# RWKV-5 attention followed by a balanced expert layer on one core: the first expert's list and gather move ahead of a branch, and the attention's preparation returns into its arm

## The chip, the core and the metric

The kernel runs on one core of a Trainium2 chip. A core has five engines with their own instruction queues: TensorE (PE, whose weight loads are shown as PEld), VectorE (DVE), ScalarE (ACT), GpSimd (POOL) and SyncE (SP), which here only issues transfers. ACT and POOL issue transfers too. The time of a run is the device's time in microseconds; the kernel before has a median of 490.0 us over three runs (488.75 to 490.1).

## The reference

Two layers follow each other. The first is a linear attention with a decaying state, for 4 batches, 8 heads, 768 steps and heads of 48 numbers. The second sends each of the resulting 3072 tokens to one of 8 experts, each of which gets exactly 384.

```python
for t in range(S):
    kt, vt, rt = (k[:, :, t], v[:, :, t], r[:, :, t])
    cur = np.einsum('bhd,bhe->bhde', u[None] * kt, vt)
    y[:, :, t] = np.einsum('bhd,bhde->bhe', rt, state + cur)
    state = w[None, :, :, None] * state + np.einsum('bhd,bhe->bhde', kt, vt)
...
x = attn_out.transpose(0, 2, 1, 3).reshape(B * S, H * D)
logits = x @ w_gate
for idx in np.argsort(-logits.flatten()):
    tok, e = (int(idx) // E, int(idx) % E)
    if assigned[tok] >= 0 or counts[e] >= cap:
        continue
    assigned[tok] = e
    counts[e] += 1
...
for e in range(E):
    mask = assigned == e
    h = np.maximum(x[mask] @ w1[e], 0.0)
    out[mask] = h @ w2[e]
```

So a pair of token and expert with a high logit is served first, and an expert that has 384 tokens takes no more. An expert that has filled up is closed, its tokens are struck out, and the rest of the tokens look again among the experts left. All is 32-bit floating point.

## The kernel before, in words

**The attention** works in 24 units, each of 128 steps of one batch with all 8 heads. Heads lie in pairs, each padded to 64 columns, so that a pair fills 128. For a unit n the parts are:

- `load(n)` brings k, r and v (192 KB each) with three transfers on SP's queue.
- `scale(n)` multiplies k by powers of w (`ks`, L395, VectorE), forms the sums r·u·k by head (`rk` on POOL, L398 and L399; `dd` on VectorE, L401), and fills the diagonal of `AT` from `dd` with eight instructions on ScalarE (L404).
- `turn(n)` transposes r and ks by pairs of heads on TensorE (L414, L417). VectorE multiplies the turned r by powers of w as it takes it out of PSUM (L419), ScalarE copies the turned k (L421).
- `pairs(n)` multiplies both (g, 16 products, L460) and puts the upper triangle into `AT` (masking, L463, VectorE).
- `outputs(n)` sums state times r (L475) and AT times v (L479) into y_ps, with weights of 48 columns; ScalarE copies it to `xT` (L482). The state takes up `kv_ps` (L490, L496, L497), for all but a batch's last chunk.
- `rows(n)` turns xT back (L506), ScalarE copies it (L508), and SP stores it to `x_rows`. `gate(c)` computes the logits of a chunk of all batches.

Iteration n of the loop (L528) traces scale(n+2), turn(n+1), pairs(n+1), outputs(n) and rows(n-1). The order on each engine's queue is not the order of the text: a planner draws it at compiling, with its own costs of instructions, from what is ready. A branch (`tc.If`) is for the planner one piece that other work may stand before or behind, but not inside. `tc.issue_after(ins)` puts instructions behind `ins` on its engine.

The class `Mild` prepares tables from w: `up` on VectorE and `ch` on POOL, both by doubling (L334 to L342), a reciprocal (L343), and a table `wk` turned by TensorE (L360). It also holds scale(0), turn(0) and scale(1), ahead of the branch that asks whether w lies in a range; here it does, and `attention_mild` is the arm that runs.

**The experts.** For each expert `walk.fill()` makes a search, the likely one (`likely`): three rounds of 16 thresholds. In each, VectorE compares (`ind`, line L706 of a helper, as are many others), TensorE counts (L718, then L729), VectorE sums in between (`own`, `cnt`, `wide`). Out of the last come the expert (`fmax`), its tokens (`acc`), their places and a flag that says whether the search is sure. Then:

1. Every engine reads the flag and takes the branch (L742); only if it is 0, `surely` searches by bits.
2. `tokens(place)` turns places into a list `tok` (L944 to L973), with VectorE and two groups of products on TensorE.
3. `leave` strikes the expert and its tokens out of the logits (L755 to L760).
4. `fetch` gathers 3 x 128 rows of `x_rows` by `tok` (POOL, L1043), and has SP read the expert's number and load w1 (L1035) and w2 (L1037), 1.5 MB each, one behind the other on SP's queue.

`turn(xg)` transposes the rows (L1053, L1054), `hidden` makes the first layer (L1062, L1063), `result` the second (L1069, L1071), and POOL scatters the rows to the output (L1072). The search, the list and the fetch of expert n+1 are traced ahead of `hidden` of expert n. Before the first expert there is nothing to lie beside.

Of the kernel before, what the change touches and what calls it, by code (L numbers as in the profile page):

```python
# [10 lines left out]
F32 = mybir.dt.float32  # L11
BF16 = mybir.dt.bfloat16
F16 = mybir.dt.float16
I32 = mybir.dt.int32
# [12 lines left out]
def attention_any(ctx, kpads, rpads, tc, r, k, v, w, u, wg, x_dram, LG, ident, walk):  # L27
# [22 lines left out]
    NB = len(kpads)  # L50
# [224 lines left out]
class Mild:  # L275
# [6 lines left out]
    def __init__(self, ctx, tc, r, k, v, w, u, wg, ident):  # L282
# [9 lines left out]
        self.tc, self.r, self.k, self.v, self.ident = tc, r, k, v, ident  # L292
        const = self.const = ctx.enter_context(tc.tile_pool(name="m_const", bufs=1))
        self.pool = ctx.enter_context(tc.tile_pool(name="m_work", bufs=2))
        self.units = [(b, c) for c in range(C) for b in range(B)]
        self.loaded, self.live, self.marks = {}, {}, {}

        flat = w.rearrange("h d -> (h d)")
        row = const.tile([1, DX], F32, name="row")
        wp = const.tile([P2, 8, HP], F32, name="wp")  # L300
        nc.vector.memset(wp[:, 0, :], 1.0)
        with nc.allow_non_contiguous_dma(reason="a row to the partitions"):
            for q in range(2):
                nc.scalar.dma_start(wp[q * PD:q * PD + D, 0, :], w.rearrange("(a q) d -> q d a", q=2)[q])
        nc.sync.dma_start(row, flat.unsqueeze(0))


        self.vts, self.rts, self.kss = (
            [const.tile([128, H, PD], F32, name=f"{name}{i}") for i in range(n)]
            for name, n in (("vt", 8), ("rt", 6), ("ks", 4)))  # L310
        for i in range(8):
            for t in (self.rts, self.vts, self.kss):
                if i < len(t):
                    (nc.vector if i < 2 else nc.gpsimd).memset(t[i][:, :, D:PD], 0.0)
        self.wg_sb = const.tile([128, HP, 32], F32, name="wg_sb")
        nc.vector.memset(self.wg_sb, 0.0)
# [3 lines left out]
        for n in range(1, 4):  # L320
            self.load(n)
        for q in range(2):
            nc.scalar.dma_start(self.wg_sb[q * PD:q * PD + D, :, 0:E],
                                wg.rearrange("(a q d) e -> q d a e", q=2, d=D)[q])

# [19 lines left out]
        self.wr = const.tile([P2, HP, T], F32, name="wr")  # L345
        nc.scalar.copy(self.wr, ch[:, :, T + 1:1:-1])
        self.wp = wp
        mask = const.tile([128, 128], F32, name="mask_f")
        make_upper_triangular(nc, mask, val=1.0, diag=False)
        self.mask = const.tile([128, 128], U8, name="mask")  # L350
        nc.gpsimd.tensor_copy(self.mask, mask)

# [762 lines left out]
```

## Time and profile before

| | before |
|---|---|
| median of runs | 490.0 us (488.75 to 490.1) |
| profiled execution | 490.1 us |
| its span, first to last instruction | 488.4 us |
| TensorE busy, instructions | 420.4 us (86%), 2896 |
| VectorE busy | 199.7 us (41%) |
| ScalarE busy | 149.7 us (31%) |
| POOL busy | 120.3 us (25%) |
| first product g of unit 0 starts | 17.36 us |
| last unit's xT copied out of PSUM | 173.19 us |
| first search starts (m) | 179.04 us |
| first expert product starts | 210.44 us |
| read from HBM, written | 44.25 MB, 9.44 MB |

The profile is of one execution. Its times count from the first instruction, so that the span lies some 1.7 us below the execution's own time. The attention goes to about 175 us, the handover from 179 to 210, the eight experts from there to the end. Waits are put down to what released them; idle time on an engine that others do not wait for costs nothing.

### The profile page before, as it was taken

The page shows a single profiled execution, that of the slowest core. Times are in us where ns is not written, and L with a number is a line of the kernel's source. Part 1 is how long each engine was busy: PE and PEld are TensorE (multiplying, and loading weights), DVE is VectorE, ACT ScalarE, POOL GpSimd, SP SyncE. Part 2 cuts the span into 40 slices and gives each one's busy share as a digit, 9 for nine tenths or more (in the row PEclk, how much of TensorE's full clock was granted, in tenths as well). Part 3 has the DMA queues.
Part 4 walks back from the last instruction along what each step waited for, and adds up shares of the span by engine and source line. Part 5 has one row for each costly group of instructions (what it writes and reads, how often), then busy time and mean ns, then how long its engine had stood idle before and what let it go on. Part 6 is the DMA issues. An engine that isn't in the chain of part 4 may idle for free. (4 is left out here: it accounts for less than half of the span.)

```text
span 488.4 us, 7858 instructions
## 1 busy us (share of the span) xinstructions
PE 420.4 (86%) x2896; PEld 275.2 (56%) x2896; DVE 199.7 (41%) x673; ACT 149.7 (31%) x389; POOL 120.3 (25%) x178
## 2 busy tenths in 40 slices
PE   0798989899988631189999999999999999999994
PEld 0677767777776520145655655655656556556552
DVE  6775657555663327444045064072270350300000
ACT  2845546655556510012121121121221221212210
POOL 5914563444440000202102102203103112201001
PEclk9999999999999975569999999999999999999999
DMA  8986545555201010716203505307209019510000
GB/s 163 200 165 140 122 109 107 124 127 126 71 34 36 33 39 1 261 46 237 103 17 129 212 17 209 132 17 279 77 2 322 32 52 398 182 32 32 17 16 32
DMA packets 93960, 54.36 MB, mean 111 GB/s; under 512 B 77137, under 2 KB 88530, under 8 KB 93906
## 3 DMA queue, kind: packets, MB, share of 16 engines
q1 hardware_dynamic: 89858, 44.05, 32.1%
q0 software_dynamic: 3072, 9.44, 5.3%
q8 instruction: 27, 0.44, 0.4%
q10 hardware_dynamic: 976, 0.21, 0.3%
q14 instruction: 27, 0.22, 0.1%
HBM read 44.25 MB, written 9.44 MB: 110 GB/s over the span
## 5 line engine op out<-in xcount | busy, mean ns | idle before, releaser
L1062 PE MATMUL h_ps<-xT,w 128*128 128x384 f32 x384 | 137.5, 506 | 1.4 <-ACT xT L1054 0.5
L1069 PE MATMUL o_ps<-w,hid 128*128 128x384 f32 x384 | 127.5, 486 | 0.0
L1069 PEld LDWEIGHTS o_ps<-w,hid 128*128 128x128 f32 x384 | 71.9, 190 | 47.2
L1062 PEld LDWEIGHTS h_ps<-xT,w 128*128 128x128 f32 x384 | 69.5, 194 | 45.9 <-issue 10.6
L404 ACT ACTIVATE AT<-ident,dd 128x128 f32<-128x128 f32 x192 | 58.6, 388 | 59.2 <-PE y_ps L479 59.2
L1063 ACT ACTIVATE hid<-h_ps 128x384 f32<-128x384 f32 x64 | 31.4, 491 | 109.5 <-PE h_ps L1062 107.1
L1043 POOL DMA_INDIRECT xg<-x_rows,tok x24 | 23.3, 971 | 161.9 <-PE h_ps L1062 63.5
L1072 POOL DMA_INDIRECT out_dram<-o_sb,tok x24 | 23.7, 989 | 127.6 <-ACT o_sb L1071 122.4
L706 DVE TENSOR_TENSOR own<-counts,same 128x64 f32<-128x64 f32 x21 | 4.7, 225 | 102.0 <-PE counts L718 102.0
L1071 ACT COPY o_sb<-o_ps 128x384 f32<-128x384 f32 x24 | 11.5, 479 | 108.3 <-PE o_ps L1069 100.2
L475 PE MATMUL y_ps<-rT,state 128*48 128x128 f32 x320 | 31.0, 287 | 13.6 <-ACT xT L482 13.6
L398 POOL TENSOR_TENSOR rk<-rt,kt 128x384 f32<-128x384 f32 x24 | 24.8, 1033 | 66.7 <-DVE dd L401 38.8
L463 DVE COPY_PREDICATED AT<-mask,g_ps 128x512 f32<-128x512 uint8 x48 | 32.3, 725 | 19.4 <-ACT AT L404 17.8
L479 PE MATMUL y_ps<-AT,vt 128*48 128x128 f32 x384 | 32.8, 281 | 0.0
L475 PEld LDWEIGHTS y_ps<-rT,state 128*48 128x48 f32 x320 | 20.0, 126 | 20.9 <-issue 13.8
L460 PE MATMUL g_ps<-rT,kT 48*128 48x128 f32 x384 | 28.8, 291 | 2.3 <-DVE AT L463 1.5
L460 PEld LDWEIGHTS g_ps<-rT,kT 48*128 48x128 f32 x384 | 24.2, 193 | 7.0 <-issue 6.7
L479 PEld LDWEIGHTS y_ps<-AT,vt 128*48 128x48 f32 x384 | 25.1, 126 | 1.4 <-ACT xt L508 0.4
L399 POOL TENSOR_TENSOR rk<-rk,u_bc 128x384 f32<-128x384 f32 x24 | 25.6, 1070 | 0.5
L395 DVE TENSOR_TENSOR ks<-kt,wk 128x384 f32<-128x384 f32 x24 | 18.1, 762 | 13.6 <-PE kv_ps L490 13.5
L414 PE MATMUL rT_ps<-ident,rt 128*128 128x128 f32 x96 | 16.7, 297 | 6.3 <-DMA rt<-in_r_dram 6.3
L1054 ACT COPY xT<-xT_ps 128x384 f32<-128x384 f32 x24 | 10.9, 486 | 35.9 <-PE counts L718 32.1
(170 smaller groups left out, 405.2 us busy)
## 6 DMA issues: line engine op xcount, KB each, us to landing
w<-in_moe_w_dram SPq DMA_DIRECT2D x16, 1536.0 KB, 7.4
kt<-in_k_dram SPq DMA_DIRECT2D x24, 192.0 KB, 3.0
rt<-in_r_dram SPq DMA_DIRECT2D x24, 192.0 KB, 3.2
vt<-in_v_dram SPq DMA_DIRECT2D x24, 192.0 KB, 3.4
x_rows<-xt SPq DMA_DIRECT2D x24, 192.0 KB, 1.9
xg<-x_rows,tok POOLq DMA_INDIRECT x24, 6.3
out_dram<-o_sb,tok POOLq DMA_INDIRECT x24, 2.6
u_bc<-in_u_dram ACTq DMA_DIRECT2D x1, 192.0 KB, 3.7
```

The source lines that it names most:

```text
L398: nc.gpsimd.tensor_mul(rk, rt[:, :, 0:D], kt)
L399: self.marks["rk"] = nc.gpsimd.tensor_mul(rk, rk, self.u_bc.rearrange("p (h d) -> p h d", h=H)).ins
L404: nc.scalar.activation(AT[:, h % 2, h // 2, :], self.ident, AF.Copy, scale=dd[:, h:h + 1])
L460: g = nc.tensor.matmul(g_ps[:, q, a, :], kT[halves[q], a, :], rT[halves[q], a, :], start=True, stop=True)
L463: marks["AT"] = nc.vector.copy_predicated(out=AT[:, q], mask=mask.unsqueeze(1).to_broadcast([128, HP, T]), data=g_ps[:, q]).ins
L475: nc.tensor.matmul(y_ps[halves[q], a, :], S0[:, a, q, 0:D], rT[:, a, :], start=(a == 0), stop=False, skip_group_check=True)
L479: nc.tensor.matmul(y_ps[halves[q], a, :], vt[:, 2 * a + q, 0:D], AT[:, q, a, :], start=(c == 0 and a == 0), stop=(a == HP - 1), skip_group ...
L1043: nc.gpsimd.indirect_dma_start(out=xg[:, c, :], out_offset=None, in_=x_dram, in_offset=bass.IndirectOffsetOnAxis(ap=tok[:, c:c + 1], axis=0))
L1062: nc.tensor.matmul(h_ps, w1[:, f, ts(j, 128)], xT[:, f, :], start=(f == 0), stop=(f == KD - 1))
L1063: nc.scalar.activation(hid[:, j, :], h_ps, AF.Relu)
L1069: nc.tensor.matmul(o_ps, hid[:, j, ts(c, 128)], w2[:, j, :], start=(j == 0), stop=(j == KF - 1))
L1072: nc.gpsimd.indirect_dma_start(out=out_rows[n * NC + c], out_offset=bass.IndirectOffsetOnAxis(ap=tok[:, c:c + 1], axis=0), in_=o_sb, in_of ...
```

## The change

It has two sides. On the experts' side:

- `tokens` and the gather (now `rows`) are traced ahead of reading the flag, for the likely search's places, and once more inside the branch's arm, into the same tiles, behind `surely`.
- `leave` follows the branch, and thus the list.
- In `likely`, `eq`, `low`, `base`, `em` and `past_low` are put behind `ind` or `wide` (`issue_after`), where VectorE waits for counts; the flag goes behind `place`.
- For the first expert alone, w2 is issued by ScalarE, behind the copy of the first turned rows, and not by SP behind w1.

On the attention's side:

- scale(0), scale(1) and turn(0) go from `Mild`, ahead of the branch, into `attention_mild`.
- r is scaled on VectorE before it is turned (`rs`, from a table `wr` that is turned like `wk`), and ScalarE copies the turned r. The rows `xt` are copied by VectorE instead of ScalarE.
- y_ps is written with weights of 64 columns, pads included, and is allocated in each unit; its one memset goes.
- In `Mild`, 12 pads are cleared on VectorE (before, 18 on VectorE and POOL), w's transfer `wp` is traced behind them, behind the mask and behind the filling of the states. Three units are loaded ahead, not four; v has 6 tiles, not 8.
- `attention_any` makes its own padded tiles; this arm does not run.

The diff, cut to its core:

```diff
+        self.vts, self.kss, self.rss = (
+            [const.tile([128, H, PD], F32, name=f"{name}{i}") for i in range(n)]
+            for name, n in (("vt", 6), ("ks", 4), ("rs", 2)))
+        for t in self.vts + self.kss + self.rss:
+            nc.vector.memset(t[:, :, D:PD], 0.0)
...
+        self.state = [const.tile([128, HP, 2, PD], F32, name=f"state{b}") for b in range(B)]
+        for t in self.state:
+            nc.scalar.activation(t.rearrange("p a q d -> p a (q d)"),
+                                 ident.unsqueeze(1).to_broadcast([128, HP, 128]), AF.Copy, scale=0.0)
+        self.wg_sb = const.tile([128, HP, 32], F32, name="wg_sb")
+        nc.vector.memset(self.wg_sb, 0.0)
         flat = w.rearrange("h d -> (h d)")
...
         wp = const.tile([P2, 8, HP], F32, name="wp")
         nc.vector.memset(wp[:, 0, :], 1.0)
         with nc.allow_non_contiguous_dma(reason="a row to the partitions"):
             for q in range(2):
                 nc.scalar.dma_start(wp[q * PD:q * PD + D, 0, :], w.rearrange("(a q) d -> q d a", q=2)[q])
...
-        self.vts, self.rts, self.kss = (
-            [const.tile([128, H, PD], F32, name=f"{name}{i}") for i in range(n)]
-            for name, n in (("vt", 8), ("rt", 6), ("ks", 4)))
-        for i in range(8):
-            for t in (self.rts, self.vts, self.kss):
-                if i < len(t):
-                    (nc.vector if i < 2 else nc.gpsimd).memset(t[i][:, :, D:PD], 0.0)
-        self.wg_sb = const.tile([128, HP, 32], F32, name="wg_sb")
-        nc.vector.memset(self.wg_sb, 0.0)
         self.u_bc = const.tile([128, DX], F32, name="u_bc")
         self.load(0)
         nc.scalar.dma_start(self.u_bc, u.rearrange("h d -> (h d)").partition_broadcast(128))
-        for n in range(1, 4):
-            self.load(n)
         for q in range(2):
             nc.scalar.dma_start(self.wg_sb[q * PD:q * PD + D, :, 0:E],
                                 wg.rearrange("(a q d) e -> q d a e", q=2, d=D)[q])
+        for n in range(1, 3):
+            self.load(n)
...
-            self.scale(0)
-            self.turn(0, ps)
-            self.scale(1)
...
+        turned = const.tile([P2, HP, T], F32, name="turned")
+        nc.scalar.copy(turned, ch[:, :, T + 1:1:-1])
+        self.wp, self.scales = wp, []
+        with tc.tile_pool(name="m_ps", bufs=2, space=PSUM) as ps, ExitStack() as part:
+            for name, t in (("wk", ch), ("wr", turned)):
+                sc_ps = ps.tile([128, HP, P2], F32, name="sc_ps")
+                for a in range(HP):
+                    nc.tensor.transpose(sc_ps[:, a, :], t[:, a, 0:T], ident[0:P2, 0:P2])
+                sc = const.tile([128, DX], F32, name=name)
+                nc.scalar.copy(sc.rearrange("p (h d) -> p h d", h=H),
+                               sc_ps.rearrange("p a (q d) -> p (a q) d", q=2)[:, :, 0:D])
+                self.scales.append(sc)
...
-        nc.vector.tensor_mul(ks[:, :, 0:D], kt, self.wk.rearrange("p (h d) -> p h d", h=H))
...
-        rT = pool.tile([128, HP, T], F32, name="rT", bufs=3)
-        nc.vector.tensor_mul(rT, rT_ps, self.wr)
-        kT = pool.tile([128, HP, T], F32, name="kT")
-        nc.scalar.copy(kT, kT_ps)
...
-    halves = [slice(q * PD, q * PD + D) for q in range(2)]
-    y_ps = ps.tile([128, HP, T], F32, name="y_ps")
-    nc.vector.memset(y_ps, 0.0)
-    turned = {}
...
+    def scale(n):
+        load(n + 3)
+        kt, rt, vt = loaded.pop(n)
+        ks, rs = kss[n % 4], rss[n % 2]
+        nc.vector.tensor_mul(ks[:, :, 0:D], heads(kt), heads(wk))
+        nc.vector.tensor_mul(rs[:, :, 0:D], heads(rt), heads(wr))
+        rk = pool.tile([128, DX], F32, name="rk")
+        nc.gpsimd.tensor_mul(rk, rt, kt)
+        marks["rk"] = nc.gpsimd.tensor_mul(rk, rk, u_bc).ins
+        dd = pool.tile([128, H], F32, name="dd")
+        nc.vector.tensor_reduce(out=dd, in_=heads(rk), axis=AX.X, op=ALU.add)
+        AT = pool.tile([128, 2, HP, T], F32, name="AT", bufs=3)
+        for h in range(H):
+            nc.scalar.activation(AT[:, h % 2, h // 2, :], ident, AF.Copy, scale=dd[:, h:h + 1])
+        live[n] = dict(vt=vt, ks=ks, rs=rs, AT=AT)
+    def turn(n):
+        ks, rs = live[n]["ks"], live[n]["rs"]
+        kT_ps = ps.tile([128, HP, T], F32, name="kT_ps")
+        for a in range(HP):
+            nc.tensor.transpose(kT_ps[:, a, :], pair(ks, a), ident)
+        rT_ps = ps.tile([128, HP, T], F32, name="rT_ps")
+        for a in range(HP):
+            nc.tensor.transpose(rT_ps[:, a, :], pair(rs, a), ident)
+        kT = pool.tile([128, HP, T], F32, name="kT")
+        nc.scalar.copy(kT, kT_ps)
+        rT = pool.tile([128, HP, T], F32, name="rT", bufs=3)
+        nc.scalar.copy(rT, rT_ps)
+        live[n].update(kT=kT, rT=rT)
...
+        y_ps = ps.tile([128, HP, T], F32, name="y_ps")
         if c > 0:
             for a in range(HP):
                 for q in range(2):
-                    nc.tensor.matmul(y_ps[halves[q], a, :], S0[:, a, q, 0:D], rT[:, a, :],
+                    nc.tensor.matmul(y_ps[halves[q], a, :], S0[:, a, q, :], rT[:, a, :],
                                      start=(a == 0), stop=False, skip_group_check=True)
         for a in range(HP):
             for q in range(2):
-                nc.tensor.matmul(y_ps[halves[q], a, :], vt[:, 2 * a + q, 0:D], AT[:, q, a, :],
+                nc.tensor.matmul(y_ps[halves[q], a, :], vt[:, 2 * a + q, :], AT[:, q, a, :],
...
-                        nc.tensor.matmul(kv_ps[halves[q], a, :], ks[:, 2 * a + q, 0:D], vt[:, 2 * a + q, 0:D],
+                        nc.tensor.matmul(kv_ps[halves[q], a, :], ks[:, 2 * a + q, :], vt[:, 2 * a + q, 0:D],
...
-        nc.scalar.copy(xt.rearrange("p (h d) -> p h d", h=H),
-                       xr_ps.rearrange("p a (q d) -> p (a q) d", q=2)[:, :, 0:D])
+        nc.vector.tensor_copy(heads(xt), xr_ps.rearrange("p a (q d) -> p (a q) d", q=2)[:, :, 0:D])
...
+    scale(0)
+    scale(1)
+    turn(0)
     pairs(0)
     for n in range(N):
         if n + 2 < N:
-            mild.scale(n + 2)
+            scale(n + 2)
         if n + 1 < N:
-            mild.turn(n + 1, ps)
+            turn(n + 1)
...
-        tt(ind, self.by_token(m, ND), self.by_expert(cand), ALU.is_ge)
+        self.asked = tt(ind, self.by_token(m, ND), self.by_expert(cand), ALU.is_ge)
...
+        self.summed = tt(wide, digit_of.unsqueeze(2).to_broadcast([128, ND, E]),
...
         flag = self.likely(**out)
+        tok, listed = self.tokens(out["place"])
+        got = fetch(tok)
         found = nc.values_load(flag[0:1, 0:1], min_val=0, max_val=1,
                                skip_runtime_bounds_check_because="a truth value")
         with self.tc.If(found < 1):
             with ExitStack() as part:
                 pool = part.enter_context(self.tc.tile_pool(name="surely", bufs=1))
                 self.surely(pool, **out)
-        tok = self.tokens(out["place"])
+            self.tokens(out["place"], tok)
+            fetch(tok, got)
         self.leave(out["fmax"], out["acc"])
-        return out["fmax"], tok
+        return out["fmax"], tok, got
...
             if g == 0:
-                eq = pool.tile([128, NT, E], F32, name="eq")
-                tt(eq, prop, self.by_expert(self.first_e), ALU.mult)
-                em = pool.tile([128, NT], F32, name="em")
-                nc.vector.tensor_reduce(out=em, in_=eq, axis=AX.X, op=ALU.max)
+                with self.tc.issue_after(self.asked):
+                    eq = pool.tile([128, NT, E], F32, name="eq")
+                    tt(eq, prop, self.by_expert(self.first_e), ALU.mult)
+            else:
+                with self.tc.issue_after(self.asked):
+                    was, low = low, pool.tile([128, 1], F32, name="low")
+                    nc.vector.scalar_tensor_tensor(out=low, in0=self.cell[:, g - 1:g], scalar=dg, in1=was,
+                                                   op0=ALU.mult, op1=ALU.add)
+            with self.tc.issue_after(self.summed):
+                if g < 2:
+                    base = pool.tile([128, ND], F32, name="base")
+                    nc.vector.tensor_scalar(out=base, in0=self.cells[:, g + 1, :], scalar1=low, scalar2=None,
+                                            op0=ALU.add)
+                else:
+                    em = pool.tile([128, NT], F32, name="em")
+                    nc.vector.tensor_reduce(out=em, in_=eq, axis=AX.X, op=ALU.max)
+                    past_low = pool.tile([128, 1], F32, name="past_low")
+                    tt(past_low, low, self.cell[:, 2:3], ALU.subtract)
             if g < 2:
-                base = pool.tile([128, ND], F32, name="base")
-                nc.vector.tensor_scalar(out=base, in0=self.cells[:, g + 1, :], scalar1=low, scalar2=None, op0=ALU.add)
                 most = pool.tile([128, ND], F32, name="most")
...
-                was, low = low, pool.tile([128, 1], F32, name="low")
-                nc.vector.scalar_tensor_tensor(out=low, in0=self.cell[:, g:g + 1], scalar=dg, in1=was,
-                                               op0=ALU.mult, op1=ALU.add)
...
-        flag = pool.tile([128, 1], I32, name="flag")
-        nc.vector.scalar_tensor_tensor(out=flag, in0=upto[:, NT - 1:NT], scalar=float(CAP), in1=n_sole,
-                                       op0=ALU.is_equal, op1=ALU.mult)
-        tt(upto, upto, st_ps[:, 1, :], ALU.add)
-        nc.vector.scalar_tensor_tensor(out=place, in0=upto, scalar=128.0, in1=acc, op0=ALU.add, op1=ALU.mult)
+        before = pool.tile([128, NT], F32, name="before")
+        tt(before, upto, st_ps[:, 1, :], ALU.add)
+        placed = nc.vector.scalar_tensor_tensor(out=place, in0=before, scalar=128.0, in1=acc,
+                                                op0=ALU.add, op1=ALU.mult).ins
+        with self.tc.issue_after(placed):
+            flag = pool.tile([128, 1], I32, name="flag")
+            nc.vector.scalar_tensor_tensor(out=flag, in0=upto[:, NT - 1:NT], scalar=float(CAP), in1=n_sole,
+                                           op0=ALU.is_equal, op1=ALU.mult)
...
+    def rows(tok, xg=None):
+        if xg is None:
+            xg = xpool.tile([128, NC, DX], F32, name="xg")
+        for c in range(NC):
+            nc.gpsimd.indirect_dma_start(
+                out=xg[:, c, :], out_offset=None, in_=x_dram,
+                in_offset=bass.IndirectOffsetOnAxis(ap=tok[:, c:c + 1], axis=0))
+        return xg
+    def fetch(fmax, tok, xg, late=False):
         number = xpool.tile([1, 1], I32, name="number")
         nc.vector.tensor_scalar(out=number, in0=fmax[0:1, :], scalar1=-1.0, scalar2=float(E),
                                 op0=ALU.mult, op1=ALU.add)
-        e = nc.values_load(number[0:1, 0:1], engines=(mybir.EngineType.SP,), min_val=0, max_val=E - 1,
+        queues = (mybir.EngineType.SP, mybir.EngineType.Activation)
+        e = nc.values_load(number[0:1, 0:1], engines=queues if late else queues[:1], min_val=0, max_val=E - 1,
                            skip_runtime_bounds_check_because="E less a number from 1 to E")
         w1 = wpool.tile([128, KD, F], F32, name="w1")
         nc.sync.dma_start(w1, moe_w1[ds(e, 1)].rearrange("o (c p) f -> p (o c) f", p=128))
         w2 = wpool.tile([128, KF, DX], F32, name="w2")
-        nc.sync.dma_start(w2, moe_w2[ds(e, 1)].rearrange("o (c p) d -> p (o c) d", p=128))
-        return w1, w2
...
-    def turn(xg):
+        queue = nc.scalar if late else nc.sync
+        second = lambda: queue.dma_start(w2, moe_w2[ds(e, 1)].rearrange("o (c p) d -> p (o c) d", p=128))
+        if not late:
+            second()
+        return xg, tok, w1, w2, second
+    def turn(xg, second=None):
         xT = xpool.tile([128, KD, CAP], F32, name="xT")
         for c in range(NC):
             xT_ps = ps_t.tile([128, KD, 128], F32, name="xT_ps")
             for f in range(KD):
                 nc.tensor.transpose(xT_ps[:, f, :], xg[:, c, ts(f, 128)], ident)
-            nc.scalar.copy(xT[:, :, ts(c, 128)], xT_ps)
+            copied = nc.scalar.copy(xT[:, :, ts(c, 128)], xT_ps)
+            if c == 0 and second:
+                with tc.issue_after(copied.ins):
+                    second()
...
-    ahead = fetch(*walk.fill())
-    xT = turn(ahead[0])
+    ahead = fetch(*walk.fill(rows), late=True)
+    xT = turn(ahead[0], ahead[-1])
     for n in range(E):
-        _, tok, w1, w2 = ahead
+        _, tok, w1, w2, _ = ahead
         if n + 1 < E:
-            ahead = fetch(*(walk.fill() if n + 2 < E else walk.remainder()))
+            ahead = fetch(*(walk.fill(rows) if n + 2 < E else walk.remainder(rows)))
```

## The prediction

> **What bounds the kernel now.** I read the table of stages first, then the timeline of the handover between attention and experts, then one cycle of the attention and the list of waits, last the first 18 us.
>
> The stages (columns: window, its length, then busy us and instructions of PE, PEld, DVE, ACT, POOL, granted clock, DMA share, GB/s):
>
> ```profile
> 88.00:116.00 28.00, 26.00 (x361) 20.44 (x359) 16.28 (x31) 16.91 (x52) 12.15 (x17) 1.00 0.57 124
> 180.00:190.00 10.00, 1.80 (x12) 0.82 (x13) 7.37 (x31) 0.00 (x0) 0.00 (x0) 0.50 0.00 0
> 190.00:200.00 10.00, 1.35 (x13) 0.73 (x12) 7.99 (x40) 0.00 (x0) 0.57 (x1) 0.50 0.10 20
> 200.00:210.00 10.00, 2.80 (x14) 1.92 (x13) 2.43 (x10) 1.05 (x3) 2.50 (x3) 0.50 0.94 356
> 245.00:280.00 35.00, 34.61 (x131) 19.94 (x130) 13.30 (x61) 6.61 (x14) 5.92 (x6) 1.00 0.35 125
> ```
>
> Three regimes. From 210 on, TensorE works 34.6 of 35 us for each expert: nothing on other engines can shorten it. From 179 to 210 nothing overlaps: VectorE chooses the first expert's tokens, then DMA brings rows and weights. Up to 175 the attention runs at 26 of 28 us of TensorE, so it is close to that engine but not against it.
>
> The handover:
>
> ```profile
> 191.82 0.16 DVE L828 SCALAR_TENSOR_TENSOR flag<-upto,n_sole 128x1 int32<-128x1 f32 x1
> 192.22 0.18 DVE L831 SCALAR_TENSOR_TENSOR place<-upto,acc 128x24 int32<-128x24 f32 x1
> 193.87 0.18 DVE L944 TENSOR_SCALAR lo<-place 128x24 int32<-128x24 int32 x1 [1.46 <-DVEq L742]
> ...
> 197.55 0.42 SPq L1035 DMA_DIRECT2D w<-in_moe_w_dram  x1
> ...
> 198.22 0.15 DVE L973 TENSOR_REDUCE tok<-mine 128x3 int32<-128x12 f32 x1
> ...
> 199.43 1.17 POOL L1043 DMA_INDIRECT xg<-x_rows,tok  x1 [52.43 <-DVE cnt L725]
> ...
> 206.53 0.90 PE L1053 MATMUL xT_ps<-ident,xg 128*128 128x128 f32 x3 [6.46 <-DMA xg<-x_rows,tok]
> ```
>
> The branch costs VectorE 1.46 us, the list 4.50 (193.87 to 198.37), the first gathered rows 7.10 from their issue. The first expert matmul starts at 210.44, released by the last turned rows.
>
> One attention cycle (6.45 us, or 6.97 with a gate in it):
>
> ```profile
> 107.11 2.45 ACT L404 ACTIVATE AT<-ident,dd 128x128 f32<-128x128 f32 x8 [3.03 <-PE y_ps L479]
> 108.63 0.56 DVE L395 TENSOR_TENSOR ks<-kt,wk 128x384 f32<-128x384 f32 x1 [1.32 <-PE kv_ps L490]
> 109.29 1.34 DVE L463 COPY_PREDICATED AT<-mask,g_ps 128x512 f32<-128x512 uint8 x2
> 109.46 0.56 ACT L482 COPY xT<-y_ps 128x512 f32<-128x512 f32 x1
> 110.16 1.05 PE L475 MATMUL y_ps<-rT,state 128*48 128x128 f32 x14 [0.66 <-ACT xT L482]
> 111.14 1.16 PE L460 MATMUL g_ps<-rT,kT 48*128 48x128 f32 x16
> ```
>
> A loop: outputs end (107.07), ScalarE fills AT (2.45), copies xT (0.56), TensorE runs the state products, g and the outputs (3.4). The list of waits for 32 to 150 us says the same: "ACT AT L404 <- PE y_ps L479: 50.9, 18, 3.7" and only 9.4 us of TensorE behind xT. Masking ends at 110.63, 0.5 before g.
>
> **What the skill says.** "TensorEngine Tiling (Array Packing)", Available Configurations: without row tiling a weight of up to 64 columns takes one of two 128x64 tiles, and tiles work in parallel. The trace agrees: 16 products of 48 columns and 128 moving ones take 1.2 to 1.3 us, 8 pairs of 0.15, what one transpose of the full array takes (four in 0.60). So 48 and 64 columns should cost alike. "TensorE: Matmul & The Clock Gate", LDWEIGHTS: a load costs by its columns. The rows have 126 ns for 48 columns and 190 for 128, so some 139 for 64, an estimate; the loads lie beside the matmuls. "DMA: Bandwidth & Descriptors", Queues, rings and completion order: each DMA engine takes turns between queue rows by packets. Before, both weight matrices are on one queue; no row here shows the two sharing.
>
> **The change, part by part: the experts' side.**
> - Side values: eq and em leave the front (179.82 to 180.48: 0.66); low leaves two rounds (0.13 each). They go behind ind or wide, where VectorE waits for TensorE 0.4 to 0.6 us anyway; only em with past_low (0.5) overfills the last such wait of 0.36, giving back 0.1. Flag goes behind place: 0.19, of which it takes 0.13 again ahead of the list. So the list can start at 192.40 - 0.66 - 0.26 + 0.1 - 0.19 + 0.13 = 191.5 instead of 193.87, since the branch (1.46) is behind it.
> - The list loses its fill-ins: fe 0.14, dead 0.27, m about 0.15, ind about 0.4, so 3.5 rather than 4.5. tok at 195.0 instead of 198.37.
> - Gather: POOL began 1.06 after tok here, 0.27 at the next expert. Issued at 195.3 to 196.1, I take 195.7; the others 1.25 apart. With no weights in the way I price a landing by the scatters' 2.6 (median on the page) up to 3.2: the last rows at 201, turned by 203.
> - The weights lose: VectorE passes the branch after tok (0.84 to 1.46, to 196.2), strikes out (about 1.2), SP reads the number (1.0): w1 issued at 198.4, 0.9 later. It has 1.57 MB; at 356 GB/s 4.4 and about 2 to land: 204.8. w2, issued by ScalarE behind the first turned rows (about 200.5), halves it from 201.5 in the worst case: 207.1. I take 205.8, later than xT: w1 becomes the last thing. w2 has 20 us of first-layer work over it; without that cover it would cost some 3.
> - First expert matmul at 205.8 instead of 210.4: 4.6 gained, bounds 3.3 and 6.0 (207.1, 204.4).
> - The later seven searches do the same work under 34.6 of 35 us of TensorE: nothing. Without that cover the same 4 us a search would count. The gathers issue earlier on POOL, whose queue has only scatters behind them, and these wait for o_sb. The branch's arm now lists and gathers again, but no row of it runs in this trace.
>
> **The attention's side, taken back.**
> - The head: before, w's powers are ready when wp has landed (5.95), reciprocal ends at 9.99, POOL's ch at 12.77 (rk in between), and g of unit 0 starts at 17.36, 4.6 later. After, 13 memsets of 0.14 precede wp's own, so its transfer starts near 2.9, or behind ACT's table load and four state fills (1.28 + 4 x 0.55) near 5; it lands 4.2 later, 7.2 to 9.6. 4.0 to the reciprocal and 0.4 more for ch: 11.6 to 14.0. Then one scale more is turned (1.11 + 0.48) and r multiplied before its transposes, partly beside the other, 6.2 rather than 4.6: 17.8 to 20.2, and 2.4 later if AT of unit 1 is ahead of the copies of kT and rT on ACT. Units 0 to 2 then follow as before. I take 20.0: 2.7 lost, bounds 0.4 and 5.3. The arm's branch costs nothing visible before (ACT goes from AT to AT without a gap there), up to 1.5 in the worst case, within the bounds. Loads: three units ahead instead of four; with units 6.5 apart and landings of 3.0 to 3.4 this is 19 us early: nothing.
> - The cycle: VectorE loses rT (0.69, out of PSUM), gains rs (0.56 alone; ks, its like, averages 0.76) and xt (0.48). ACT loses xt (0.48), gains rT (0.57): the order AT, xT, kT, rT ends at 111.0, still before g's 111.14. kv with 64 columns: 0.1 in TensorE's 0.66 of slack. But rs comes behind ks, and ks ends at 109.19 with masking waiting behind it: it then ends 0.56 to 0.76 later, 111.2 to 111.4, and g waits 0.15 to 0.35. In three cycles of four (in a gate cycle ks is elsewhere): 0.19 on average, times 22: 4.1 lost. Bounds: -0.66 a cycle if another order frees TensorE from xT (its idle), +0.6 if ACT's two copies come ahead of xT too: -14 and +13.
> - y_ps memset (0.48) leaves: hidden before behind kT. The last xt on VectorE instead of ACT: same 0.48.
>
> Sum: -4.6 + 2.7 + 4.1 = +2.2. On the profiled execution (490.1, span 488.4 and 1.7 around it) 492.3; the median of the runs is 490.0, hardly different.
>
> **Rivals.** Less than 0.3% (1.5 us) can't be told from no change here.
> - Main, slower: 489.5 to 496, likeliest 492.3. Chance 0.42.
> - A. The attention loop doesn't notice: rs fits before masking or behind it, and the head costs 1 to 2 as the old interleaving of rk with ch on POOL was itself slow. For it: g had 0.5 us of slack; against: ks already fills the space to masking. -4.6 + 1.5 = 487, faster. It decides when the cycle stays under 6.55. Chance 0.30.
> - B. The cycle grows by 0.4 to 0.6, as rT's copy and xT compete on ACT ahead of g: -4.6 + 2.7 + 11 = 499. For it: ACT in order is the loop's longest part; against: it idles 2.7 each cycle. Chance 0.18.
> - C. The order drawn at compiling lets AT or g of the next unit run before the outputs end: -0.5 a cycle, 490 - 11 - 2 = 477 to 483. AT has three buffers yet waits for the outputs just ended, so there is room. Chance 0.07.
> - D. The early gather brings nothing, since rows wait for the arm that may write them too and for w1 behind w2: 210 as before, with the attention's loss 495 to 497. Chance 0.03.
>
> Faster: C, A without its near-zero part, a little of main: 0.33. Within 0.3%: the meeting of A and main, 0.17. Slower: 0.50. The range of 8 in 10 leaves out C and the upper half of B: 484 to 500; the main case's own is 489.5 to 496.
>
> **What would show it.** Right: first gather near 195.7 on the shifted clock, that is 17 us after the first m instead of 20.4; first expert matmul 27 after it instead of 31.4, released by w1; g of unit 0 near 20; cycle 6.6 with g waiting for masking; experts at 34.6 of 35. Wrong: a cycle below 6.4 or above 6.9, gathers still at 7 us to landing, or an expert's period other than 34.5 to 35.

## The result and the profile after

The kernel after takes 471.32 us (median; 468.33 to 471.97) beside 489.73 us for the kernel before, a ratio of 0.9615 (95% interval 0.9571 to 0.9659). It is faster by 3.9%; 492.3 had been forecast, with a range of 484 to 500.

The profiled executions took 490.1 and 471.97 us, their spans 488.4 and 470.2. I cut both spans at the same five events, read from the timelines: the end of the last output product of unit 3 and of unit 23, the first search's first instruction (m), the first expert product.

| stretch | before | after | difference | forecast |
|---|---|---|---|---|
| start to the outputs of unit 3 | 39.50 | 44.53 | +5.0 | +2.7 |
| 20 cycles, units 4 to 23 | 133.07 (6.65 each) | 113.09 (5.65 each) | -20.0 | +4.1 for 22 |
| outputs of unit 23 to m | 6.47 | 5.71 | -0.8 | 0 |
| m to the first expert product | 31.40 | 32.02 | +0.6 | -4.6 |
| first expert product to the end | 277.95 | 274.88 | -3.1 | 0 |
| sum | 488.4 | 470.2 | -18.2 | +2.2 |

All of the gain and more is in the attention's cycle. Of the other four stretches, the handover (m to the first expert product) went the other way from what I had written, and the experts, for which I had forecast nothing, gained 3.1 us.

**The stages after**, in the columns of the table of before (window, length, busy us and instructions of PE, PEld, DVE, ACT, POOL, clock, DMA share, GB/s):

```profile
88.00:116.00 28.00, 26.68 (x399) 23.82 (x396) 21.66 (x41) 18.23 (x52) 17.79 (x21) 1.00 0.64 137
164.00:174.00 10.00, 1.79 (x12) 0.82 (x13) 8.12 (x34) 0.00 (x0) 0.00 (x0) 0.50 0.01 2
174.00:184.00 10.00, 1.09 (x11) 0.87 (x11) 7.07 (x33) 0.00 (x0) 3.00 (x3) 0.50 0.13 28
184.00:194.00 10.00, 2.85 (x14) 1.64 (x13) 2.45 (x10) 1.44 (x3) 0.27 (x1) 0.50 0.93 348
245.00:280.00 35.00, 34.85 (x138) 20.06 (x137) 14.51 (x63) 6.60 (x14) 5.95 (x6) 1.00 0.35 125
```

The busy time of TensorE in the first window hardly moved (26.00 to 26.68 of 28), but it issued 399 matmuls where there were 361. I had read 26 of 28 as close to the engine's limit; a busy PE had not meant a PE at its peak.

**One cycle after**, from the timeline:

```profile
82.61 0.58 ACT L492 COPY xT<-y_ps 128x512 f32<-128x512 f32 x1 [2.76 <-PE y_ps L489]
83.09 2.45 ACT L444 ACTIVATE AT<-ident,dd 128x128 f32<-128x128 f32 x8
83.73 1.34 DVE L472 COPY_PREDICATED AT<-mask,g_ps 128x512 f32<-128x512 uint8 x2
84.41 1.09 PE L485 MATMUL y_ps<-rT,state 128*64 128x128 f32 x16
85.44 0.57 ACT L457 COPY kT<-kT_ps 128x512 f32<-128x512 f32 x1
85.90 0.58 ACT L459 COPY rT<-rT_ps 128x512 f32<-128x512 f32 x1
86.54 1.16 PE L469 MATMUL g_ps<-rT,kT 48*128 48x128 f32 x16
```

Before, ScalarE filled AT (2.45) and only then copied xT, so the state products waited for both. Now xT comes first, AT is filled behind it, for a unit three further on (unit 12, beside the xT of unit 9), whose masking comes only at 95.14. The lists of waits over the cycles say where the loop went. The first line before (32 to 165 us; total, times, longest):

```profile
ACT AT L404 <- PE y_ps L479: 56.5, 20, 3.7
```

The first two after (32 to 140 us):

```profile
POOL rk L438 <- DMA rt<-in_r_dram: 37.4, 17, 7.7
ACT xT L492 <- PE y_ps L489: 29.2, 10, 4.9
```

AT's wait for the output products is gone; where ScalarE waits for them now, it is to copy xT. Why AT waited can be read from the addresses of the built program. Before, `Mild` allocates AT with bufs=3 in a pool that is opened outside the branch, and fills units 0 and 1 ahead of the branch. Those two buffers are read inside the arm, and in the arm they are never given out again: AT of all the units 2 to 23 has one address. After, the pool is opened in the arm and three addresses rotate. (kT too has one address before, and rT two; e3 below leaves these as they are.)

**The head**, ScalarE's rows of the timeline of after:

```profile
15.28 0.58 ACT L457 COPY kT<-kT_ps 128x512 f32<-128x512 f32 x1 [1.27 <-PE kT_ps L452]
18.30 4.79 ACT L444 ACTIVATE AT<-ident,dd 128x128 f32<-128x128 f32 x16 [2.44 <-DVE dd L441]
23.00 0.56 ACT L459 COPY rT<-rT_ps 128x512 f32<-128x512 f32 x1
```

g of unit 0 starts at 23.61 (17.36 before). r is turned by 16.05, but ScalarE's queue has sixteen AT fills ahead of the copy, and the first of them waits for dd until 18.30.

**The handover after:**

```profile
175.47 0.18 DVE L856 SCALAR_TENSOR_TENSOR place<-before,acc 128x24 int32<-128x24 f32 x1
...
175.68 0.18 DVE L975 TENSOR_SCALAR lo<-place 128x24 int32<-128x24 int32 x1
...
179.17 0.17 DVE L1005 TENSOR_REDUCE tok<-mine 128x3 int32<-128x12 f32 x1
180.39 1.16 POOL L1064 DMA_INDIRECT xg<-x_rows,tok  x1 [38.23 <-DVEq L760]
...
182.44 0.43 SPq L1077 DMA_DIRECT2D w<-in_moe_w_dram  x1
183.13 1.14 POOL L1064 DMA_INDIRECT xg<-x_rows,tok  x1 [0.30 <-issue]
183.71 0.90 PE L1090 MATMUL xT_ps<-ident,xg 128*128 128x128 f32 x3 [4.78 <-DMA xg<-x_rows,tok]
...
190.06 0.87 PE L1090 MATMUL xT_ps<-ident,xg 128*128 128x128 f32 x3 [3.14 <-issue]
...
193.96 0.34 PE L730 MATMUL counts<-prop,ind 128*128 128x64 bf16 x3 [1.66 <-DVE ind L718]
...
195.25 0.27 PE L741 MATMUL counts<-wide,ones_h 128*128 128x128 f16 x1 [0.94 <-DVE wide L718]
195.35 0.98 PE L1103 MATMUL h_ps<-xT,w 128*128 128x384 f32 x1
```

The list is 3.34 us earlier after m (its last step starts at 15.84 instead of 19.18), and the first rows take 3.3 us instead of 7.1. The third rows, issued when the weights start, take 6.9. xT is complete at 191.45, yet the first product starts at 195.35, right behind counts of the next search, which the planner had put ahead of it in TensorE's queue.

### The profile page after: what moved, and what is told of

Read it like the earlier page. It is cut to its first block, busy times and chain, and to the rows that moved or that the text cites. A ratio compares the mean times of both kernels' runs of the same rounds, so it can differ in the third digit from the quotient of the medians.

```text
span 470.2 us, 7886 instructions
## 1 busy us (share of the span) xinstructions
PE 410.9 (87%) x2900; PEld 278.1 (59%) x2900; DVE 218.4 (46%) x702; ACT 153.3 (33%) x390; POOL 123.4 (26%) x166
## 5 line engine op out<-in xcount | busy, mean ns | idle before, releaser
L1103 PE MATMUL h_ps<-xT,w 128*128 128x384 f32 x384 | 135.6, 503 | 0.1
L438 POOL TENSOR_TENSOR rk<-rt,kt 128x384 f32<-128x384 f32 x24 | 26.0, 1084 | 42.5 <-DMA rt<-in_r_dram 37.4
L489 PE MATMUL y_ps<-AT,vt 128*64 128x128 f32 x384 | 30.5, 281 | 0.0
L492 ACT COPY xT<-y_ps 128x512 f32<-128x512 f32 x24 | 14.0, 585 | 39.8 <-PE y_ps L489 36.8
L489 PEld LDWEIGHTS y_ps<-AT,vt 128*64 128x64 f32 x384 | 25.3, 140 | 0.9 <-issue 0.4
L485 PE MATMUL y_ps<-rT,state 128*64 128x128 f32 x320 | 25.7, 282 | 0.0
L507 POOL TENSOR_TENSOR state<-state,wp 64x192 f32<-64x192 f32 x32 | 18.9, 590 | 14.0 <-DVE state L506 12.8
L441 DVE TENSOR_REDUCE dd<-rk 128x8 f32<-128x384 f32 x24 | 13.1, 545 | 17.8 <-POOL rk L439 16.1
```

Of the source, the lines that this page charges most:

```text
L438: nc.gpsimd.tensor_mul(rk, rt, kt)
L485: nc.tensor.matmul(y_ps[halves[q], a, :], S0[:, a, q, :], rT[:, a, :], start=(a == 0), stop=False, skip_group_check=True)
L489: nc.tensor.matmul(y_ps[halves[q], a, :], vt[:, 2 * a + q, :], AT[:, q, a, :], start=(c == 0 and a == 0), stop=(a == HP - 1), skip_group_c ...
L1103: nc.tensor.matmul(h_ps, w1[:, f, ts(j, 128)], xT[:, f, :], start=(f == 0), stop=(f == KD - 1))
```

## The experiments

In the first four runs the kernel before has a median of 489.73 us beside the variants, in the next four 489.05, in the last three 490.22. The table has each variant's median, its ratio to the kernel before, and from its profile the end of unit 3's outputs, the mean of 20 cycles, m to the first expert product, and from there to the end.

| run | us | ratio (95%) | y3 | cycle | m to h | h to end |
|---|---|---|---|---|---|---|
| before | 489.73 | 1 | 39.50 | 6.65 | 31.40 | 277.95 |
| after | 471.32 | 0.9615 (0.9571 to 0.9659) | 44.53 | 5.65 | 32.02 | 274.88 |
| e1 experts only | 489.06 | 0.9986 (0.9961 to 1.001) | 40.67 | 6.66 | 31.77 | 275.09 |
| e2 attention only | 472.68 | 0.9659 (0.9601 to 0.9716) | 42.29 | 5.64 | 31.59 | 278.16 |
| e3 before, AT in the arm | 467.11 | 0.9551 (0.9503 to 0.9598) | 37.26 | 5.58 | 31.30 | 277.59 |
| e4 after, one AT | 504.23 | 1.0301 (1.0254 to 1.0349) | 53.71 | 6.91 | 31.80 | 275.48 |
| e5 after, 48 columns | 471.93 | 0.9642 (0.9583 to 0.9702) | 46.21 | 5.61 | 32.06 | 275.17 |
| e6 after, r on VectorE | 479.14 | 0.9834 (0.9765 to 0.9903) | 46.24 | 5.78 | 32.25 | 274.34 |
| e7 after, turn(0) first | 469.08 | 0.9595 (0.9545 to 0.9646) | 44.46 | 5.67 | 31.84 | 275.57 |
| e8 after, h first | 466.38 | 0.9542 (0.9486 to 0.9598) | 42.51 | 5.69 | 28.08 | 275.76 |
| e9 after, list behind | 473.37 | 0.9658 (0.9617 to 0.9699) | 42.41 | 5.59 | 33.40 | 277.95 |
| e10 after, two AT | 490.11 | 0.9990 (0.9972 to 1.0009) | 47.19 | 6.34 | 31.91 | 274.49 |
| e11 combined | 460.66 | 0.9398 (0.9365 to 0.9431) | 37.37 | 5.55 | 28.17 | 275.64 |

**e1 and e2: which half.** e1 is the kernel before with the change's expert half (list and gather, `issue_after`, w2's queue), e2 with its attention half.

```diff
# e1, against before; e2 has the rest of the change instead
+        tok, listed = self.tokens(out["place"])
+        got = fetch(tok)
...
-        tok = self.tokens(out["place"])
+            self.tokens(out["place"], tok)
+            fetch(tok, got)
```

> The kernel before with the experts' side of the change alone. The prediction on record: 4.6 us faster, 485. From the two traces instead: first search to first expert product 0.6 us longer, the experts behind it 3.1 us shorter, so about 487, 2.5 us faster; an expert's period 33.7 us instead of 34.2.

> The kernel before with the attention's side of the change alone. The prediction on record: 6.8 us slower, 497. From the two traces instead: head 5 us longer, cycle of a unit 1.0 us shorter twenty times, the arm left 0.8 us sooner: about 474, 16 us faster. The two sides alone should add up to the whole change, 18 us.

The attention half alone brings 3.4%. The expert half alone brings nothing that its interval can tell from zero, where 2.5 us had been expected; its profile has the experts 2.9 us shorter, but the outputs of unit 3 1.2 us later.

**e3 and e4: the buffers of AT.** e3 is the kernel before, with AT from unit 2 on in a pool of the arm, and nothing else of the change; e4 is the kernel after with one buffer for AT.

```diff
# e3, against before
+        self.arm = None
...
-        AT = pool.tile([128, 2, H // 2, T], F32, name="AT", bufs=3)
+        AT = (self.arm or pool).tile([128, 2, H // 2, T], F32, name="AT", bufs=3 if self.arm else 2)
...
+    mild.arm = pool
# e4, against after
-        AT = pool.tile([128, 2, HP, T], F32, name="AT", bufs=3)
+        AT = pool.tile([128, 2, HP, T], F32, name="AT", bufs=1)
```

> The kernel before; from unit 2 on AT is allocated from a pool opened inside the arm, with three buffers, and nothing else is changed (weights of 48 columns, r scaled as it leaves PSUM, xt on ScalarE, units 0 and 1 ahead of the branch all stay). Theory of the buffers (units 0 and 1 keep two of AT's three buffers for the whole arm, because they are allocated ahead of the branch and used in it): a cycle of 5.6 to 5.8 us instead of 6.65, AT no longer released by y_ps, 469 to 472. Rival of the engines (the gain comes from r's and xt's other engines): no change, 489 to 490. Rival of the columns: no change.

> The kernel after, with one buffer for AT instead of three. Theory of the buffers: AT waits for the outputs just ended again, a cycle of 6.5 to 6.7 us, 488 to 492. Rival of the engines, rival of the columns: 471, or little above.

Three lines in the kernel before bring a cycle of 5.58 us, with the head, the scaling of r and the copies on ScalarE as they were. One buffer in the kernel after makes it 6.91, 12 us more in all than I had expected (the outputs of unit 3 alone end 9.2 later than in the kernel after), and the wait is back at the top of the list (32 to 190 us):

```profile
ACT AT L444 <- PE y_ps L489: 70.1, 22, 7.2
```

**e10: two buffers.** The same edit as e4 with bufs=2.

> The kernel after with two AT buffers in the arm in place of three. Theory of the buffers with TensorE as the next bound (96 of 100 us busy with three): with two, AT of unit n+2 waits for the outputs of unit n, which leaves one unit of lead: the cycle is 5.6 to 6.0 us, 471 to 479 us. Rival (each buffer less costs alike; one buffer gave 6.91, three 5.65): 6.1 to 6.4 us, 481 to 488 us.

The mean cycles, 6.91, 6.34 and 5.65 us for one, two and three buffers, look as if each buffer were worth some 0.6 us, as the rival had it. But the time, 490.11 us, is above both ranges, and the steady part of the loop says something else:

| usable buffers | run | mean of units 4 to 23 | units 12 to 19 |
|---|---|---|---|
| one | before | 6.65 | 6.58 |
| one | e4 | 6.91 | 6.61 |
| two | e10 | 6.34 | 6.55 |
| three | after | 5.65 | 5.59 |
| three | e3 | 5.58 | 5.57 |

There a second buffer brings next to nothing, and the third brings the whole gain. The 0.6 us between e4 and e10 come from units 4 to 11 (7.38 and 6.50 a unit; the profile of e4 has a stretch at half the clock there, 79.3 to 86 us) and from the last four (6.60 and 5.60).

Why two are not enough stands in the timeline of e10. Its list of waits (32 to 150 us) has no name for what AT waits for:

```profile
ACT AT L444 <- issue: 42.3, 17, 3.1
```

But it is the outputs again:

```profile
104.74 1.04 PE L489 MATMUL y_ps<-AT,vt 128*64 128x128 f32 x16
105.91 2.44 ACT L444 ACTIVATE AT<-ident,dd 128x128 f32<-128x128 f32 x8 [2.47 <-issue]
108.26 0.56 ACT L492 COPY xT<-y_ps 128x512 f32<-128x512 f32 x1
```

These outputs are of unit 12 and the fill is of unit 14, which takes unit 12's buffer; in nearly all units from 4 to 23 the fill starts 0.1 us behind the outputs of two units before. Ahead of xT in ScalarE's queue, it keeps xT, and with it the next state products, waiting for 2.4 us, as in the kernel before. With three buffers the one that comes free at these outputs goes to the unit three further on, and its fill stands behind xT. The kernel's text agrees: it has `scale(n+2)` ahead of `outputs(n)`, `scale(n+3)` behind. That the planner follows the text in this, and whether xT put ahead of the fill would do as much with fewer buffers, was not tested.

**e5 and e6: columns and engines.** e5 gives the kernel after weights of 48 columns and a y_ps that is cleared once; e6 turns r raw and lets VectorE scale it out of PSUM.

```diff
# e5, against after
-    halves = [slice(q * PD, q * PD + PD) for q in range(2)]
+    halves = [slice(q * PD, q * PD + D) for q in range(2)]
+    y_ps = ps.tile([128, HP, T], F32, name="y_ps")
+    nc.vector.memset(y_ps, 0.0)
# e6, against after
-        nc.vector.tensor_mul(rs[:, :, 0:D], heads(rt), heads(wr))
...
-        nc.scalar.copy(rT, rT_ps)
+        nc.vector.tensor_mul(rT, rT_ps, mild.turned)
```

> The kernel after with weights of 48 columns and one cleared y_ps for the whole arm, as before. Theory of the buffers (the cycle shortened because AT fills ahead): the columns cost or bring nothing, 470 to 473 us, cycle 5.6 to 5.7 us; y_ps single in both, its users' order unchanged. Rival, the columns (64-column weights, or y_ps taken anew for every unit, shorten the cycle): the cycle returns part of the way to 6.65, so 475 to 490 us.

> The kernel after, but r is turned raw and multiplied by its scale on VectorE as it leaves PSUM, as before, instead of being scaled ahead of the turn and copied on ScalarE; the AT buffers stay in the arm. Theory of the buffers: the cycle stays near 5.6 us (5.5 to 5.9), and the first g comes some 2 us earlier because rT no longer stands behind AT fills on ScalarE: 467 to 474 us. Rival, the engines (moving r's exit from PSUM to ScalarE is what shortened the cycle): the cycle is 6.2 to 6.7 us, 483 to 492 us.

The columns cost nothing: 471.93 us and 5.61 a cycle. In e6 the cycle is 5.78, and e3, where VectorE also scales r as it leaves PSUM, has 5.58; so the engine of r's copy did not make the change's gain. But e6 is 8 us slower than the kernel after, above its expectation. Its profile shows 1.7 us to unit 3 and 2.5 over 20 cycles; the rest isn't in that one profiled execution (476.04 us, the fastest of four). e6 also has POOL read r from padded tiles, but its rk takes no longer there (1055 ns, 1084 in the kernel after). What makes e6 slower stays open.

**e7: the head.**

```diff
     scale(0)
-    scale(1)
     turn(0)
+    scale(1)
```

> The kernel after with the turn of unit 0 traced ahead of the scaling of unit 1, as before. Theory of the head (g of unit 0 comes at 23.6 instead of 17.4 us because the copy of rT stands behind sixteen AT fills in ScalarE's queue and now stands behind eight, of 0.29 us each): g at 20.5 to 21.5 us, cycle unchanged at 5.6, and 468 to 470 us. Rival (the head is long because the scales' own work and the branch come first, or the first outputs wait for something else): g or the outputs of unit 3 do not move, 470.5 to 472.5 us.

g of unit 0 came at 21.10, as expected, 2.5 earlier and behind eight fills, but the outputs of unit 3 end at 44.46, where the kernel after has 44.53, and e2, e8 and e9, with the same head as the kernel after, have 42.3 to 42.5. The profiled execution of e7 is the slowest of its five (472.57 us). The median, 469.08, is in the expected range, but its interval overlaps that of the kernel after. The cause of the late g is shown; that it is what delays the attention is not.

**e8: the order on TensorE's queue.** The first hidden group of the first expert is traced ahead of the second search, and that search's counts are queued behind it.

```diff
+        with (self.tc.issue_after(self.behind) if self.behind else ExitStack()):
+            for j in range(NT // G):
+                nc.tensor.matmul(each.rearrange("p i e -> p (i e)"),
...
-    def hidden(w1, xT):
+    def hidden(w1, xT, hid=None, js=range(KF)):
...
+        early = 1 if n == 0 else 0
+        hid = hidden(w1, xT, js=range(early)) if early else None
```

> The kernel after with the first hidden group of the first expert issued ahead of the second search's counts on TensorE. Theory of the queue (the first hidden product waits 3.9 us behind two rounds of counts though its rows are turned): first product 28 to 28.8 us after the first search begins instead of 32.0, and the end 2 to 4 us earlier, 467 to 469.5 us. Rival (the counts fill a hole that the weights leave, w1 or the rows being late): the first product moves by less than 1 us, or what it gains is lost in the first expert's period, which waits for the later list: 470.5 to 473 us.

The first product comes 28.08 us after m, right behind the last copy of xT, with six products before the first counts:

```profile
188.50 0.87 PE L1094 MATMUL xT_ps<-ident,xg 128*128 128x128 f32 x3 [2.51 <-issue]
189.95 4.21 PE L1108 MATMUL h_ps<-xT,w 128*128 128x384 f32 x6 [0.57 <-ACT xT L1095]
193.95 0.36 PE L732 MATMUL counts<-prop,ind 128*128 128x64 bf16 x3
```

Of the 3.9 us, 0.9 is lost again in the first expert's period (36.94 instead of 36.04); but that period is 35.6 to 36.7 in the other kernels that have the order of the kernel after, so how much of it the order costs is not settled. The profiled span is 4.5 below that of the kernel after: 3.0 by this, 2.0 by a shorter head, of which more below, less 0.7 in the stretches between.

**e9: the list.** The list and the gather are traced behind the branch again.

```diff
-        tok, listed = self.tokens(out["place"])
-        got = fetch(tok)
         found = nc.values_load(flag[0:1, 0:1], min_val=0, max_val=1,
...
-            self.tokens(out["place"], tok)
-            fetch(tok, got)
+        tok, listed = self.tokens(out["place"])
+        got = fetch(tok)
         self.leave(out["fmax"], out["acc"])
```

> The kernel after with the list and the gather traced behind the branch again, and not in its arm, but still ahead of the striking out; the side values stay in the waits and the first second weights stay behind the first rows. Theory of the list (TensorE stood some 0.5 us for the list in every period, because the list came behind the branch): periods near 34.2 us instead of 33.73, 3 us over six of them, and the first list 1 to 3 us later; 473 to 477 us. Rival (the side values or the other edits of the search took the 0.5 us away): periods stay at 33.7 to 33.8, 470.5 to 473 us.

The expert periods go back to 34.4 us from 33.73, and the list comes 2.2 us later after m. TensorE's waits in the periods (245 to 445 us) show the two places, its pass through the branch and the list:

```profile
PE h_ps L1101 <- PEq L758: 1.4, 4, 0.4
PE some_ps L985 <- DVE vals L718: 1.3, 4, 0.4
```

In the kernel before, its list of the same window has "PE some_ps L956 <- DVE vals L706: 1.4, 4, 0.4", and in the kernel after neither is there. e9 keeps the side values as they are in the kernel after, so they are not what took this wait away.

**e11: what brings something, together.** The kernel before with e3's buffers, the expert half and e8's order; the attention's head stays as before.

> The kernel before with AT from unit 2 on in three buffers of the arm, all of the change's expert part, and the first hidden group of the first expert ahead of the second search's counts; the head stays as before. If the three gains add: 467.1 (the buffers alone) less 3 (periods) less 3 to 5 (first product) = 459 to 462 us, cycle 5.6, first product at +28 to +28.8 us, periods 33.7. Rival (the earlier first product is paid back in the first expert's period): 463 to 466 us.

460.66 us: the gains add. It is 6.0% below the kernel before and some 2.3% below the kernel after. It is also 5.7 us below e8, and its outputs of unit 3 end 5.1 earlier (37.37 and 42.51): the head that the change brought is a loss.

## Why the prediction was wrong

- **The cycle** ("another order frees TensorE from xT" at one end, "4.1 lost" taken; measured -20.0). The working carried the loop of before, outputs, AT, xT, state products, into the kernel after, and only moved copies between engines in it. The step that failed is the assumption that AT's wait stays. The sign was in the view that I quoted, AT waiting 50.9 us for outputs that had just ended, and rival C even said so ("AT has three buffers yet waits for the outputs just ended, so there is room"). But C took it for a matter of the drawn order alone, at -0.5 a cycle and 0.07. It began with where the pool is opened: one usable buffer instead of three, 1.07 us a cycle in e3. A wait that the declared number of buffers rules out should have been traced to its cause before any sum was made; the diff has that allocation in plain view.
- **rs ahead of masking** (0.19 a cycle lost): no such loss is seen. rs stands at 82.80 to 83.34, ahead of masking at 83.73, but g now comes at 86.54, 1.5 us behind masking's end.
- **64 columns, y_ps in each unit** (nothing): right, e5. The Trainium skill's "TensorE: Matmul & The Clock Gate", LDWEIGHTS, has a load cost by its columns, and the estimate of 139 ns for 64 columns is 140 on average for the loads of y_ps from v in the profile after.
- **The head** (+2.7): g of unit 0 is 6.25 us later, not 2.7, since rT's copy stands behind sixteen fills ("2.4 later if AT of unit 1 is ahead of the copies" was in the bounds and left out of the sum). At the outputs of unit 3 the term looks near: 5.0 later here, 2.8 to 3.0 in e2, e8 and e9, which have the same head. That is luck. The 39.50 of before already has AT's wait in it. With the head of before and three buffers (e3 and e11) these outputs end at 37.3, so e2, e8 and e9 are some 5 us later, about twice the term; 2 us more of this execution are a longer cold start (below).
- **The list, the gather and the weights** were right: tok done 16.0 us after m (15.96 forecast), first gather 17.06 (17), first rows 3.3 us after their issue (2.6 to 3.2), w1 issued 19.1 after m (19.4).
- **The first expert product** (-4.6, measured +0.6): xT was complete 28.1 us after m, later than the forecast 24, as the third rows, beside the weights, took 6.9 us; and then the product waited 3.9 us more behind counts. "Released by w1" fails at TensorE's queue: I priced data and left out who stands ahead on the engine. e8 shows it: 3.9 us earlier, 3.0 of them kept to the end.
- **The later searches** ("nothing"; -3.1): TensorE's 34.6 of 35 us hid a wait for the list of some 0.5 us in each of five periods, which the order list, branch, strike removes (e1, e9); the other 0.7 us is in the first period. A share of 99% left 1% to gain in each expert.
- **Rivals.** A and B fall with the cycle. D had the time of the first product (no gain) but not the reason: the first rows came 3.3 us after their issue. The range missed because C had the right place and half the size.

## What to carry to other kernels

Where an engine waits for a buffer although the declaration says that there are several, ask which of them can be reused there: a tile allocated ahead of a branch and read in its arm kept its buffer for the whole arm, in this program, and a pool opened inside the arm gave all three back. Find what each wait in the loop is *for* before pricing copies that move within it. Buffers need not pay one by one: in the steady loop two were worth no more than one here, and the third 1.0 us a cycle, as only with it did the fill come behind the copy that the next products wait for. And when data is made to arrive earlier, read what stands ahead of its user in that engine's queue; 3.3 us won by the list were lost there, and a change of the order won them.

## What the runs showed that was not expected

TensorE starts slowly, and for how long differs between executions. Four transposes take 1.09 us at 14.11 in the profile after and 0.60 at 83.44. The products of g of unit 1 take 2.08 us at 29.18 in it, and 1.16 in e8 at 28.96, whose first g starts within 0.2 us of that. From that first g on TensorE is busy nearly without a break in both (9.59 of 9.60 us from 23.60 in the profile after). In the profile after, single products of 128 columns take 421 ns as late as 32.7 us, and 273 from 33.34; in e8 they take 272 from 29.17. The windows of e8 show the granted clock rise there:

```profile
23.40:28.80 5.40, 5.37 (x42) 4.36 (x42) 3.06 (x6) 3.39 (x10) 2.09 (x3) 0.50 0.38 74
28.90:33.30 4.40, 4.40 (x68) 3.83 (x68) 2.90 (x6) 2.71 (x8) 0.38 (x1) 1.00 0.65 128
```

The trace of after has its first clock record at 33.30, so its windows say nothing of the time before. The Trainium skill's "TensorE: Matmul & The Clock Gate", Part 1: The HAM clock gate, puts the change about 4 us into sustained work, give or take 0.5. Here it comes 9.7 and 5.4 us behind the first g: both are longer, and they differ by more than that. The two timelines are 0.2 us apart at 29 us and 2.0 apart from 33 on, up to the end of unit 3's outputs (44.53 and 42.51); that is about what e7 was meant to measure.

The gathered rows took 3.3 us alone and 6.9 beside the weights, in a window in which all transfers moved 348 GB/s.
